# Memory attention in front of two expert layers: attention worked by whole batches instead of half batches

## The chip, the cores and the metric

One core of a Trainium2 chip runs the whole program. The metric is the device time of one execution in microseconds; lower is better. Times of a kernel are given as the median of several runs, and one further execution was profiled.

## What is computed

q, k and v have the shape (4 batches, 8 heads, 576 tokens, 64), phi has (4, 8, 576, 32). For each batch and head:

```
a    = softmax(phi, axis=2)                 # over the 576 tokens
k_m, v_m = a^T k, a^T v                     # 32 memory rows of 64
attn = softmax(q k_m^T / 8)                 # over the 32 memory rows
out  = attn v_m
```

The result, as 2304 tokens by 512, goes through a first layer (512 to 2048, leaky ReLU, back to 512; its weights are float64) and through a second one of 4 experts (512 to 1024, ReLU, back to 512), whose outputs are summed with the token's normalised domain probabilities as weights.

## The kernel before

**The order of the work.** The body does not issue instructions at once. It gives each operation to a planner (`Plan.op`, L52) with an engine, a cost in us, a due time, and the tiles and PSUM banks that it reads and writes. `Plan.issue` (L94) then simulates the engines with these costs, takes in each queue the operation that is ready and due first, and emits it. So each engine's order is fixed before the run, by costs and due times; at run time an engine works its list strictly in order. SP's list holds the DMA issues; it too is worked in order.

**Attention.** A group is 4 heads of one batch, so there are 8 groups, two for each batch (`att_group`, L519). Its steps: phi (L531 to L543: the whole group is transposed in 32x32 blocks by VectorE, the maximum over tokens is taken, ScalarE takes the exponential and the sum), a (L552: six TensorE transposes back to token layout and a copy), q (L558: a block transpose of the group's queries), kv (L569: 24 products of 96 tokens each), k (L581 to L601: scaling, transposes, copies), and scores (L615: 24 products, and then L627 to L651 on VectorE, ScalarE and GpSimd: block transpose, maximum, subtraction, exponential, sum, reciprocal, product, transpose back). At the end `split` (L335, L338) writes the tokens as a rounded high part and a remainder. q, k and v come in as one DMA each for a group: 96 partitions with 4 rows of 1536 bytes (6 tokens). phi comes in on 128 partitions with rows of 2304 bytes. The dues of the loads are in `LOADS` and `order` (L220, L672 to L697).

**First layer.** It runs in steps (`moe1_step`, L930): one step is a half batch (288 tokens) and 128 of the hidden columns. In a step there are 6 products on L895 (into the hidden layer), a leaky ReLU on L950, a `split`, and 12 products on L962 to L964 (out of the hidden layer, 4 of each line). What L895 multiplies with, the product of v_m and the weights, is made in `y_pair` (L897, matmuls on L911). The first unit covers 6 column chunks: for each batch 12 steps, six for the first 288 tokens and six for the other 288. The four batches of this unit come first, in order.

**Weights.** The float64 weights are turned into float32 on the chip, a piece of 128x512 values at a time (`piece64`, L782): ScalarE L795 and L799, VectorE L807 and L810, GpSimd L815 or L819, for w_out a `split` as well. A piece lands in one of three raw buffers (`RAWS`, L212; `raw_piece`, L716). A w_in piece is two DMAs of 64 partitions (L733). The first unit needs 6 pieces of w_in and 6 of w_out, 512 KB each.

**Idle products.** While TensorE has nothing to do in the first 50 us of the plan, the planner puts in products of the identity with itself (L471), whose results nobody reads.

**Tokens.** A token's column is (c, position) with 6 consecutive tokens on a row, so the probabilities and the result are moved with a stride, in two or three DMAs for each 128 tokens (L388, L1158).

Of the kernel before, what the change touches and what calls it, by code (L numbers as in the profile page):

```python
# [12 lines left out]
U32 = mybir.dt.uint32  # L13
# [162 lines left out]
def kernel(  # L176
# [197 lines left out]
    def rows_of(dram, b, c, lo, n):  # L374

        return dram[b * S:(b + 1) * S, :].rearrange("(p c) w -> c p w", c=NC)[c, lo:lo + n, :]

    def pieces(t):

        done = 0  # L380
        while done < P:
            b, s = divmod(t * P + done, S)
            c, lo = divmod(s, PC)
            n = min(P - done, PC - lo)
            yield done, b, c, lo, n
            done += n

    def load_probs(t):  # L388
        for at, b, c, lo, n in pieces(t):
            nc.sync.dma_start(out=pr[at:at + n, t, :], in_=rows_of(moe2_domain_probs, b, c, lo, n))  # L390
# [78 lines left out]
    def idle(bank):  # L469
# [5 lines left out]
    W = HG * NC * D  # L475
    pl = [tile_([NR, M]) for i in range(2)]
    ql = [tile_([HG, NC, D]), xx[:, 2, S:S + W].rearrange("p (h c d) -> p h c d", h=HG, c=NC)]
    kv = [tile_([2, HG, NC, D]), xx[:, 0:2, S:S + W].rearrange("p i (h c d) -> p i h c d", h=HG, c=NC)]
    eT = tile_([S])
    qT = [exact(HG, NC, 2, M), xx[:, 3, S:S + W].rearrange("p (h c e t) -> p h c e t", h=HG, c=NC, e=2)]  # L480
    kb = tile_([2, P])
    a = tile_([NC, P])
    kk = exact(2, NA3, M)
    vv = exact(2, D)
    at = [tile_([NR, M + 1]) for i in range(2)]
    aT = tile_([S])
    small = {
        nm: [tile_([n]) for i in range(2)]
        for nm, n in (("mx", NR), ("sm", NR), ("nmx", 1), ("z", 1), ("rz", 1))
    }  # L490
# [5 lines left out]
    memset(["vv"], vv)  # L496
    for i in range(2):
        memset([f"one{i}"], at[i][:, :, M:M + 1], 1e-9)

    def load(nm, t, src, i, due):  # L500

        b, g = divmod(i, NGB)
        hs = slice(g * HG, (g + 1) * HG)

        def fn():
            if nm[0:2] == "pl":
                nc.sync.dma_start(
                    out=t.rearrange("p r m -> p (r m)"),
                    in_=src[b, hs, :, :].rearrange("h (t r) m -> (h t) (r m)", t=M),
                )  # L510
            else:
                nc.sync.dma_start(
                    out=t[0:PC].rearrange("p h c d -> p h (c d)"),
                    in_=src[b, hs, :, :].rearrange("h (p c) d -> p h (c d)", c=NC),
                )

        plan.op("SP", 1.0 if nm[0:2] == "pl" else 2.0, due, fn, writes=[nm])

    def att_group(i):  # L519


        b, g = divmod(i, NGB)
        x = int(i in ALT)
        pl_ = pl[i % 2]
        nmx, z, rz, mx, sm = [small[nm][i % 2] for nm in ("nmx", "z", "rz", "mx", "sm")]
        at_ = at[i % 2]
# [4 lines left out]
        op("DVE", dve(S), due, lambda: nc.vector.transpose(out=eT, in_=pl_.rearrange("p r m -> p (r m)")),  # L531
           [f"pl{i % 2}"], ["eT"])
        op("DVE", dve(S), due, lambda: nc.vector.tensor_reduce(
            out=nmx, in_=eT, axis=AX.X, op=ALU.max, negate=True), ["eT"], [f"nmx{i % 2}"])
        op("ACT", 0.93, due, lambda: nc.scalar.activation(
            out=pl_.rearrange("p r m -> p (r m)").rearrange("p (c t r) -> p r c t", c=NC, r=NA3),
            in_=eT.rearrange("p (r c t) -> p r c t", r=NA3, c=NC),
            func=AF.Exp, bias=nmx, scale=1.0, accum_out=z),
           [f"nmx{i % 2}", "eT"], [f"pl{i % 2}", f"z{i % 2}"])

        def fn():
            nc.vector.tensor_scalar_add(rz, z, 1e-9)
            nc.vector.reciprocal(rz, rz)  # L543
        op("DVE", 0.3, due, fn, [f"z{i % 2}"], [f"rz{i % 2}"])

        due = yield
        pa = Banks(psum, 2)

        def fn():
            flat = pl_.rearrange("p r m -> p (r m)")  # L550
            for c in range(NC):
                nc.tensor.transpose(pa[c * P:(c + 1) * P][0:PC], flat[:, c * PC:(c + 1) * PC], ident)  # L552
        op("PE", 0.8, due, fn, [f"pl{i % 2}", "ident"], [pa], ["a"])
        op("ACT", act(NC * P), due, lambda e: copy(e, a[0:PC].rearrange("p c m -> p (c m)"), pa[0:NC * P][0:PC]), [pa], ["a"],
           also=("DVE", dve(NC * P)))

        due = yield
        op("DVE", 1.75, due, lambda: nc.vector.transpose(  # L558
            out=qT[x][0:PC].rearrange("p h c e t -> p (h c e t)"), in_=ql[x][0:PC].rearrange("p h c d -> p (h c d)")),
           [f"ql{x}"], [f"qT{x}"])  # L560

        due = yield
        pkv = Banks(psum, 1)

        def fn():
# [643 lines left out]
```

## Time and profile before

| what | us |
|---|---|
| median of 3 runs | 1163.4 (1161.43 to 1164.5) |
| the profiled execution, its own time | 1159.59 |
| its span, first to last instruction | 1157.8 |
| TensorE busy in the span | 1130.7 |
| mean granted TensorE clock | 0.991 |

The profiled execution is 3.8 us below the median of the runs. Busy time is the time in which an engine had at least one instruction under way; in the rows, L471 counts as busy too. In tables of stretches the granted clock is a share of full speed, and the DMA share is the mean busy share of the 16 DMA engines.

### The profile page before, as it was taken

What the parts mean: (1) busy time and instruction counts of PE and PEld (TensorE: products, weight loads), DVE (VectorE), ACT (ScalarE), POOL (GpSimd) and SP (SyncE); (2) the same over time, 40 slices, a digit from 0 to 9 for tenths busy, and PEclk for the clock granted to TensorE, in tenths of its full rate; (3) what the DMA queues carried; (4) which work ended last, traced back from release to release, by engine and by line L of the source; (5) the groups of instructions that cost most, each with busy time, mean ns of one, the idle gap of its engine ahead of it and who ended that gap; (6) DMA issues with size and microseconds to landing.
All of it is one profiled execution on the core that took longest, in us unless ns stands there. A gap on an engine that the chain in (4) does not pass through costs nothing.

```text
span 1157.8 us, 18008 instructions
## 1 busy us (share of the span) xinstructions
PE 1130.7 (98%) x7328; PEld 1028.5 (89%) x7328; DVE 687.2 (59%) x1259; ACT 446.6 (39%) x915; POOL 101.1 (9%) x102
## 2 busy tenths in 40 slices
PE   6799999999999999999999999999999999999998
PEld 6579899989999998889899989999998899999997
DVE  4887547853335788668686744445476654454543
ACT  4676557743344544433333423222224223222220
POOL 1542115420000000000000000000000000000000
PEclk8989999999999999999999999999999999999999
DMA  9974504410000267555534664334444553444402
GB/s 239 223 183 117 125 2 145 129 38 1 1 20 1 101 232 263 187 200 200 197 135 165 178 216 150 135 136 152 164 164 147 172 188 134 151 164 164 164 19 55
DMA packets 58836, 160.85 MB, mean 139 GB/s; under 512 B 6529, under 2 KB 33153, under 8 KB 52609
## 3 DMA queue, kind: packets, MB, share of 16 engines
q1 hardware_dynamic: 54144, 100.98, 28.4%
q0 software_dynamic: 4608, 58.72, 14.4%
q8 instruction: 57, 0.93, 0.3%
q14 instruction: 27, 0.21, 0.1%
HBM read 125.60 MB, written 34.08 MB: 138 GB/s over the span
## 4 chain that ended last, share of the span: by engine, by line
PE 92%; DMA 3%; DVE 2%; ACT 1%; POOL 1%; issue 1%; SPq 0%; POOLq 0%; ACTq 0%; DVEq 0%
PE psum L1070 30%; PE psum L1139 11%; PE psum L1140 11%; PE psum L1138 11%; PE psum L895 8%; PE psum L962 6%; PE psum L963 5%; PE psum L964 5%; PE psum L911 1%; DMA exact<-in_moe_w_out_dram 1%; DMA exact<-in_moe_w_in_dram 1%; PE psum L569 1%; DMA att<-in_v_dram 1%; PE psum L615 1%; PE psum L552 1%
## 5 line engine op out<-in xcount | busy, mean ns | idle before, releaser
L1079 DVE TENSOR_TENSOR exact<-psum,exact 128x384 f32<-128x384 f32 x336 | 184.3, 556 | 273.4 <-PE psum L1070 269.3
L1086 ACT ACTIVATE rounded<-exact 128x384 fp32r<-128x384 f32 x192 | 100.9, 525 | 286.0 <-DVE exact L1079 284.2
L338 DVE TENSOR_TENSOR rounded<-exact,rounded 128x288 fp32r<-128x288 f32 (+3 forms) x223 | 125.3, 579 | 102.6 <-ACT rounded L335 101.9
L1140 PE MATMUL psum<-late,rounded 128*128 128x512 f32 x384 | 150.7, 392 | 0.0
L1139 PE MATMUL psum<-late,rounded 128*128 128x512 f32 x384 | 150.5, 392 | 0.0
L1138 PE MATMUL psum<-late,rounded 128*128 128x512 f32 x384 | 149.3, 389 | 0.0
L1070 PE MATMUL psum<-rounded 128*128 128x384 f32 x768 | 143.5, 336 | 0.0
L1070 PEld LDWEIGHTS psum<-rounded 128*128 128x128 f32 x768 | 134.8, 188 | 2.5 <-DVE exact L1079 0.3
L895 PE MATMUL psum<-rounded 128*128 128x288 f32 x768 | 123.3, 298 | 1.5 <-DVE rounded L338 1.2
L335 ACT CAST rounded<-exact 128x288 fp32r<-128x288 f32 (+3 forms) x235 | 112.7, 497 | 16.6 <-DVE exact L757 5.5
L962 PE MATMUL psum<-rounded 128*128 128x288 f32 x384 | 116.3, 303 | 2.8 <-ACT exact L950 2.7
L895 PEld LDWEIGHTS psum<-rounded 128*128 128x128 f32 x768 | 108.9, 190 | 5.4 <-issue 3.5
L963 PE MATMUL psum<-rounded 128*128 128x288 f32 x384 | 113.4, 295 | 0.2 <-DVE rounded L338 0.2
L964 PE MATMUL psum<-rounded 128*128 128x288 f32 x384 | 113.4, 295 | 0.0
L1070 PE MATMUL psum<-late,rounded 128*128 128x384 f32 x576 | 110.1, 336 | 0.1
L1070 PEld LDWEIGHTS psum<-late,rounded 128*128 128x128 f32 x576 | 102.0, 188 | 4.4 <-DVE exact L1079 0.4
L1090 DVE SCALAR_TENSOR_TENSOR rounded<-exact,rounded 128x384 fp32r<-128x384 f32 x192 | 98.9, 551 | 11.5 <-ACT rounded L1086 11.4
L1101 ACT COPY exact<-psum 128x384 f32<-128x384 f32 x48 | 23.1, 481 | 195.7 <-PE psum L1070 195.7
L950 ACT ACTIVATE exact<-psum 128x288 f32<-128x288 f32 x128 | 52.5, 410 | 115.9 <-PE psum L895 102.3
L1140 PEld LDWEIGHTS psum<-late,rounded 128*128 128x128 f32 x384 | 72.0, 188 | 15.1
L962 PEld LDWEIGHTS psum<-rounded 128*128 128x128 f32 x384 | 72.3, 188 | 13.4 <-issue 9.2
L1139 PEld LDWEIGHTS psum<-late,rounded 128*128 128x128 f32 x384 | 72.0, 188 | 13.4
(101 smaller groups left out, 1701.5 us busy)
## 6 DMA issues: line engine op xcount, KB each, us to landing
rounded<-kept POOLq DMA_DIRECT2D x22, 1792.0 KB, 7.7
exact<-in_moe_w_dram SPq DMA_DIRECT2D x64, 512.0 KB, 5.1
kept<-rounded SPq DMA_DIRECT2D x10, 1792.0 KB, 6.7
w<-kept POOLq DMA_DIRECT2D x10, 1792.0 KB, 7.8
kept<-w SPq DMA_DIRECT2D x6, 1792.0 KB, 6.1
exact<-in_moe_w_in_dram SPq DMA_DIRECT2D x32, 256.0 KB, 5.9
exact<-in_moe_w_out_dram SPq DMA_DIRECT2D x16, 512.0 KB, 4.3
att<-in_q_dram SPq DMA_DIRECT2D x6, 576.0 KB, 5.8
```

The source lines that it names most:

```text
L335: nc.scalar.copy(out, in_) if e == "ACT" else engine(e).tensor_copy(out, in_)
L338: engine(e).tensor_tensor(out=out, in0=in0, in1=in1, op=ALU.subtract)
L895: nc.tensor.matmul(ps, lhsT=l, rhs=r, start=start and n == 0, stop=stop and n == len(seq) - 1)
L962: nc.tensor.matmul(po, lhsT=w2l[:, ds_], rhs=th, start=first, stop=False)
L963: nc.tensor.matmul(po, lhsT=w2h[:, ds_], rhs=tl, start=False, stop=False)
L964: nc.tensor.matmul(po, lhsT=w2h[:, ds_], rhs=th, start=False, stop=last)
L1070: nc.tensor.matmul(ps[k][0:TB], lhsT=l, rhs=r, start=(i == 0), stop=(i == 5))
L1079: plan.op("DVE", dve2(TB), at[k], lambda: nc.vector.tensor_tensor(out=o, in0=ps[k][0:TB], in1=other, op=ALU.add), [ps[k], ok, from_], [key])
L1086: plan.op("ACT", act2(TB), at[k], lambda: nc.scalar.activation(out=th, in_=src, func=AF.Relu), [key, *h_from[hs[c, i]]], [keys[0]])
L1138: nc.tensor.matmul(po[0:DM], lhsT=tl, rhs=w2h[:, c], start=(p == 0 and c == 0), stop=False)
L1139: nc.tensor.matmul(po[0:DM], lhsT=th, rhs=w2l[:, c], start=False, stop=False)
L1140: nc.tensor.matmul(po[0:DM], lhsT=th, rhs=w2h[:, c], start=False, stop=(p == NP2 - 1 and c == 1))
```

## The change

A batch is now worked as a whole. q, k, v and phi of a batch come in as one DMA each, on 128 partitions, with 9 tokens in a row (2304 bytes, for phi 1152). phi stays in token layout: the maximum is taken for each of the 32 columns of each partition, reduced over partitions by a TensorE transpose, spread back by a second transpose and subtracted; the sums over tokens come out of TensorE as products with two columns of ones. kv is 72 products of 64 partitions and 32 columns. Scores and all that follows are done for a half of the tokens (288) and all 8 heads at a time. k and v of most batches, and q of one, are loaded into the space that later holds the first layer's result (`xx`), and so the first layer's first result of a batch waits until that batch's space is free. Four more raw buffers (`MORE`) lie in the same space, where q and k of batch 1 are loaded later; those two loads wait for the readers of the four. A w_in piece is one DMA; probabilities and results are one DMA for 128 tokens. Dues and planner costs are new.

```diff
-    NC = 6
-    PC = S // NC
-    NA3 = PC // 32
+    LT = S // D
+    LP = P // H
-    RAWS = 3
+    RAWS, MORE = 3, 4
-    START = 40.0
-    URGENT = 40.0
+    START = 80.0
-    LOADS = [-69.0, -11.0, -9.5, 12.0, 24.0, 36.0, 48.0]
-    EACH = 2.5
-    ALT = (1, 3)
+    LOADS = [-59.9, 0.0, 10.0, 40.0]
+    PERIOD, LEAD, EACH, LAST = 32.0, 34.0, 3.0, -7.0
...
+    places = {"A": tile_([1, HG, S]), "X": xx.rearrange("p h (b s) -> p b h s", b=B)}
+    HOME = {"k": ["X0", "X3", "X1", "X3"], "v": ["X1", "X1", "X3", "X2"], "q": ["A0", "X2", "A0", "A0"]}
...
+        src, name = {"k": k, "v": v, "q": q}[what], HOME[what][b]
+        plan.op("SP", 3.5, due, lambda: nc.sync.dma_start(
+            out=home(name), in_=src[b].rearrange("h s d -> (h s d)").rearrange("(h p w) -> p h w", h=HG, p=P)),
+            writes=[name])
...
+        op("DVE", 1.25, due, lambda: nc.vector.tensor_reduce(
+            out=mr.rearrange("p (h m) -> p h m", h=HG), in_=a.rearrange("p h r m -> p h m r"), axis=AX.X, op=ALU.max),
+           [ka], ["mr"])
+        pm = Banks(psum, 1)
+        op("PE", 0.13, due, lambda: nc.tensor.transpose(pm[0:P], mr, ident), ["mr", "ident"], [pm])
+        op("DVE", 0.3, due, lambda: nc.vector.tensor_reduce(
+            out=nmx, in_=pm[0:P].rearrange("p (g t) -> p g t", g=NGB), axis=AX.X, op=ALU.max), [pm], [f"nmx{b % 2}"])
+        op("DVE", 0.25, due, lambda: nc.vector.tensor_copy(mb, nmx.unsqueeze(2).to_broadcast([P, NGB, D])),
+           [f"nmx{b % 2}"], ["mb"])
+        pb = Banks(psum, 1)
+        op("PE", 0.13, due, lambda: nc.tensor.transpose(pb[0:P], mb.rearrange("p g t -> p (g t)"), ident),
+           ["mb", "ident"], [pb])
+        op("DVE", 1.3, due, lambda: nc.vector.tensor_tensor(
+            out=a, in0=a, in1=pb[0:P].rearrange("p (h m) -> p h m", h=HG).unsqueeze(2).to_broadcast([P, HG, LT, M]),
+            op=ALU.subtract), [pb], [ka])
+        op("ACT", 1.2, due, lambda: nc.scalar.activation(out=pl[b % 2], in_=pl[b % 2], func=AF.Exp), [], [ka])
...
+        op("DVE", 2.5, due, lambda: nc.vector.transpose(
+            out=qT.rearrange("p h c e t -> p (h c e t)"), in_=home(qn)), [qn], ["qT"])
...
+                for r in range(LT * first):
+                    for h in range(HG):
+                        nc.tensor.matmul(
+                            pkv[2 * D:2 * D + NGB][h * M:(h + 1) * M], lhsT=a[:, h, r], rhs=ones,
+                            start=(r == 0), stop=(r == LT - 1),
+                        )
+                for r in range(LT):
+                    for h in range(HG):
+                        for g in range(NGB):
+                            gs = slice(g * D, (g + 1) * D)
+                            nc.tensor.matmul(
+                                pkv[g * 512:g * 512 + n * D][h * M:(h + 1) * M].rearrange("p (i d) -> p i d", i=n),
+                                lhsT=a[gs, h, r],
+                                rhs=src[gs, :, h, r * D:(r + 1) * D],
...
+        for s in range(2):
+            due = yield
+            at_, mx, sm, soon = at[s], small["mx"][s], small["sm"][s], b == s == 0
+            ps = Banks(psum, 2)
...
                 for e in range(2):
                     for h in range(HG):
-                        for j, w in enumerate(ws):
-                            rs = slice(w * M, (w + 1) * M)
+                        for g in range(NGB):
+                            rs = slice((2 * g + s) * M, (2 * g + s + 1) * M)
                             nc.tensor.matmul(
...
+                                rhs=qT[rs, h, :, e].rearrange("p r t -> p t r"),
...
+    STEP = ("phi", "q", "k", "s0", "s1")
+    STEP0 = ("phi", "k", "q", "s0", "v", "s1")
...
+            load(name[0], b, LOADS[b] + 0.1 * "pqvk".index(name[0]) - 200.0 * (name in ("p0", "k0")))
+    loads(["p0", "k0", "v0", "q0", "p1", "k1", "q1"])
...
+    for b in range(B):
+        plan.op("X", 0.0, 0.0, lambda: None, [], [f"free{b}"], room=[f"X{b}"])
...
+        if RAWS <= n < RAWS + MORE:
...
-                    after = ["alt"] if b else []
+                    after = [f"free{b}"]
...
-                    for at, b, c_, lo, n_ in pieces(tt):
...
+                    nc.sync.dma_start(out=out[tt * P:(tt + 1) * P, :].rearrange("n (k w) -> n k w", k=KD), in_=a_)
...
+    for x in range(MORE):
+        plan.ops[loaded["q1" if x < 2 else "k1"]][3].update({plan.writer[f"more{x}"], *plan.readers[f"more{x}"]})
```

## Rows read from the trace of the kernel before

**Rows 1.** The page: TensorE's busy time, and its busy tenths in 40 slices.

```profile
PE 1130.7 (98%) x7328; PEld 1028.5 (89%) x7328; DVE 687.2 (59%) x1259; ACT 446.6 (39%) x915; POOL 101.1 (9%) x102
...
PE   6799999999999999999999999999999999999998
```

**Rows 2.** Busy time by stretch: PE, PEld, DVE, ACT, POOL, clock, DMA share, GB/s.

```profile
0.00:72.00 72.00, 52.45 (x586) 44.54 (x587) 49.74 (x73) 40.87 (x79) 26.42 (x28) 0.88 1.00 240
72.00:100.00 28.00, 28.00 (x366) 24.66 (x365) 25.07 (x41) 21.34 (x48) 9.92 (x8) 1.00 0.45 105
...
160.00:440.00 280.00, 277.73 (x2118) 263.07 (x2117) 168.01 (x316) 144.54 (x312) 38.16 (x28) 1.00 0.23 75
440.00:1158.00 718.00, 712.50 (x3562) 642.60 (x3560) 412.94 (x779) 207.99 (x403) 17.16 (x32) 1.00 0.46 159
```

**Rows 3.** The same by stretch, for line 471 alone (PE, PEld, clock, DMA, GB/s).

```profile
0.00:72.00 72.00, 15.47 (x104) 14.07 (x104) 0.88 1.00 240
```

**Rows 4.** The same for line 895 alone.

```profile
0.00:72.00 72.00, 8.46 (x48) 7.60 (x48) 0.88 1.00 240
72.00:95.00 23.00, 5.17 (x33) 4.67 (x34) 1.00 0.39 91
```

**Rows 5.** The same for line 962 alone.

```profile
0.00:72.00 72.00, 7.15 (x22) 4.41 (x22) 0.88 1.00 240
72.00:95.00 23.00, 8.38 (x27) 4.88 (x26) 1.00 0.39 91
```

**Rows 6.** Waits of SP's queue up to 80 us: total, times, longest.

```profile
SPq L733 <- POOL w L815: 20.4, 5, 7.4
```

**Rows 7.** Timeline of SP: start, length, issues.

```profile
5.57 5.84 SPq L733 DMA_DIRECT2D exact<-in_moe_w_in_dram  x4
...
30.35 3.49 SPq L733 DMA_DIRECT2D exact<-in_moe_w_in_dram  x4
...
49.24 0.59 SPq L512 DMA_DIRECT2D exact<-in_v_dram  x1
```

**Rows 8.** Busy time by stretch, columns as in rows 2: three stretches that differ in row length.

```profile
58.00:60.00 2.00, 1.69 (x57) 1.17 (x56) 1.43 (x3) 0.26 (x1) 1.28 (x1) 0.80 1.03 379
2.00:4.00 2.00, 2.00 (x11) 2.00 (x10) 0.29 (x1) 0.24 (x1) 0.00 (x0) 1.00 0.88 299
10.00:16.00 6.00, 2.92 (x49) 2.56 (x50) 1.05 (x4) 0.07 (x1) 0.00 (x0) 0.62 1.11 242
```

**Rows 9.** Groups by line and shape up to 240 us: busy, mean ns, idle before.

```profile
L558 DVE STREAM_TRANSPOSE exact<-att 96x1536 f32<-96x1536 f32 x6 | 10.6, 1765 | 0.3 <-DMA att<-in_q_dram 0.3
...
L638 DVE TENSOR_REDUCE att<-att 128x18 f32<-128x576 f32 x8 | 6.0, 752 | 0.2
...
L807 DVE SCALAR_TENSOR_TENSOR exact<-exact 128x512 uint32<-128x512 uint32 x31 | 27.2, 876 | 1.3 <-ACT exact L799 0.4
...
L810 DVE TENSOR_SCALAR exact<-exact 128x512 uint32<-128x512 uint32 x32 | 25.8, 806 | 9.5 <-ACT exact L795 9.2
```

**Rows 10.** Groups by line and shape from 72 to 160 us: busy, mean ns, idle before.

```profile
L615 PE MATMUL psum<-exact,att 32*32 32x192 f32 x240 | 7.7, 326 | 0.0
...
L569 PE MATMUL psum<-att 96*32 96x128 f32 x192 | 6.1, 275 | 0.0
...
L552 PE MATMUL psum<-att 128*96 128x128 f32 x24 | 3.3, 272 | 0.0
```

**Rows 11.** Timeline of TensorE: start, length, matmuls.

```profile
13.09 2.79 PE L569 MATMUL psum<-att 96*32 96x128 f32 x48 [4.22 <-DMA att<-in_v_dram]
...
68.39 0.95 PE L895 MATMUL psum<-rounded 128*128 128x288 f32 x6
```

**Rows 12.** Timeline: first and last operation of group 0's softmax.

```profile
19.62 1.07 DVE L627 STREAM_TRANSPOSE att<-psum 128x384 f32<-128x384 f32 x2 [2.44 <-PE psum L615]
...
27.14 1.42 POOL L338 TENSOR_TENSOR rounded<-att,rounded 128x576 fp32r<-128x576 f32 x1 [1.60 <-ACT rounded L335]
```

**Rows 13.** Timeline of TensorE: the first product of the first layer.

```profile
36.39 1.81 PE L895 MATMUL psum<-rounded 128*128 128x288 f32 x12 [1.16 <-DVE rounded L338]
```

More of the change, by code (lines that the diff above doesn't have):

```diff
@@ L369, in pool @@
         return 0.1 + n * 2.33e-3
[L374 to L386, printed above, removed]
     def load_probs(t):
-        for at, b, c, lo, n in pieces(t):
-            nc.sync.dma_start(out=pr[at:at + n, t, :], in_=rows_of(moe2_domain_probs, b, c, lo, n))
+        nc.sync.dma_start(out=pr[:, t, :], in_=moe2_domain_probs[t * P:(t + 1) * P, :])
     def norm_probs():
@@ L527, in att_group, with att_batch @@
+    def att_batch(b):
+        a = pl[b % 2].rearrange("p h (r m) -> p h r m", r=LT)
+        nmx, rz = [small[nm][b % 2] for nm in ("nmx", "rz")]
+        qn = HOME["q"][b]
+        ka = f"pl{b % 2}"
         op = plan.op
         due = yield
[L531 to L534, printed above, removed]
@@ L546, in att_group @@
-        due = yield
[L547 to L557, printed above, removed]
@@ L657, in att_group @@
-        rest((0, 1))
-        if i == ALT[-1]:
-            plan.op("X", 0.0, due, lambda: None, [], ["alt"], room=["ql1", "kv1k", "kv1v", "qT1"])
-        yield
-    LATER = {i: next((j for j in range(i + 1, NG) if (j in ALT) == (i in ALT)), NG) for i in range(NG)}
-    FIRST = (
[3 rows of a table removed]
-    )
-    STEP = (("kv", 0), ("phi", 1), ("k", 0), ("scores", 0), ("a", 1), ("q", 1))
-    order = []
-    for what, i in FIRST + tuple((what, i + n) for i in range(2, NG) for what, n in STEP if i + n < NG):
-        order.append((what, i))
-        for after, then in (("kv", "lk"), ("kv", "lv"), ("q", "lq")):
-            if what == after and LATER[i] < NG:
-                order.append((then, LATER[i]))
-        if what == "a" and i + 2 < NG:
-            order.append(("lp", i + 2))
@@ new lines, in loads @@
+    def loads(names):
+        for name in names:
+            b = int(name[1])
+            loaded[name] = len(plan.ops)
+            load(name[0], b, LOADS[b] + 0.1 * "pqvk".index(name[0]) - 200.0 * (name in ("p0", "k0")))
+    loads(["p0", "k0", "v0", "q0", "p1", "k1", "q1"])
+    for b in range(B):
+        step = STEP if b else STEP0
+        for n, what in enumerate(step):
+            if b:
+                due = PERIOD * b - LEAD + n * EACH
+            else:
+                due = n / len(step) * START - 2 * START if n < len(step) - 1 else LAST
+            gens[b].send(due)
+            loads(AFTER.get((what, b), ()))
@@ L809, in signs, with add @@
                 )
+        def add(e, out):
+            cuts = [(slice(i, i + 1),) for i in range(2)] if e == "DVE" and rk[0] == "m" else [()]
+            for cut in cuts:
+                cut = (every, *cut)
+                engine(e).tensor_tensor(out=out[cut], in0=fu[cut], in1=low[cut], op=ALU.add)
         plan.op("DVE", 0.42, due, lambda: nc.vector.tensor_single_scalar(fu, fu, 3, op=ALU.logical_shift_left),
```

316 lines of the change are left out of this document (139 added, 177 removed), and 3 rows, old and new, of the table FIRST.

## The prediction

> **What bounds the kernel now.** The page comes first: TensorE is busy for 98% of the span, and only the first two of the 40 slices are below 9 tenths [rows 1]. The table by stretch says the same more sharply. From 72 us on TensorE has no gap worth the name: all of 72 to 100, 277.73 of 280 us up to 440, and 712.50 of 718 after that; up to 72 it is busy for 52.45 [rows 2]. Of these, 15.47 are idle products [rows 3], so about 37 of the first 72 us are work, at a mean clock of 0.88. The ramp is thus the only place where anything much can be won, and what is won there reaches the end one for one, because after it TensorE alone sets the pace.
>
> How far is TensorE at 72 us? Batch 0's 12 steps have 72 products on L895 and 48 on L962. At 72 us 48 and 22 of them are done [rows 4, 5]; between 72 and 95 another 27 of L962 follow. So batch 0 is through at about 95 us. I use that as the milestone: when does the new kernel have batch 0 done and batch 1's tokens ready?
>
> What holds the ramp? The DMA engines are full: share 1.00 and 240 GB/s over the first 72 us [rows 2], some 17 MB. SP's queue adds its own delay: weight loads wait 20.4 us for GpSimd to finish with one of three raw buffers [rows 6], and behind them, in the same list, stand the inputs of the next groups. The first weight loads go out at 5.57 us behind all of batch 0's inputs, and the last v of batch 1 goes out only at 49.24 [rows 7]. VectorE is the next in line: 25.07 of 28 us from 72 to 100 [rows 2], while it does nothing for most of 10 to 16 us (1.05 of 6) [rows 8].
>
> **The change part by part.**
> Transfers. Rows of 1536 bytes come in at 242 GB/s (10 to 16 us), phi's 2304-byte rows at 299, the 4 KB rows of w_out at 379 [rows 8]. q, k and v of a batch are 3.54 MB: 14.6 us before, 11.8 at the rate of phi's rows. phi's own rows shrink to 1152 bytes; no row shows that, so I bound it by 299 (no loss) and half of it (2 us lost on 0.59 MB), and take 0.8 lost, nearer to the 242 of the next larger rows. Net 2 us a batch. The Trainium skill ("DMA: Bandwidth & Descriptors", Rules for kernel authors) asks for 128 partitions and at least 1 MiB in a DMA for full bandwidth; its table (Measured) gives 341 GB/s for 1 MB, which would make it 10.4 us a batch. In the rows 96 partitions already keep all engines full (1.11), so I hold to the length of the row; the rest is a rival.
>
> Order of the loads. By the new dues phi and k of batch 0 go first, then three weight pieces, then q and v, then four weight pieces into the new buffers without waiting, and only then batch 1. So weights can be converted while VectorE and ScalarE used to stand idle, and the 20.4 us of waiting in SP's list go at least for these pieces. What is late next is batch 1, whose q and k now wait for the readers of the four buffers.
>
> VectorE. L638 shows 752 ns for 576 columns, L558 1765 for 1536 [rows 9]. A group before: seven passes of 576 columns (L531, L533, both L627 together, L638, L639, L643, L651) 5.3, the query transpose 1.8, small ones 0.8: 7.9 us, 15.8 a batch. Now: a maximum over 1152 columns 1.5, subtraction 1.5, query transpose 2304/1536 x 1.765 = 2.65, small ones 0.9, and twice (five passes of 576 plus a reciprocal, 4.0) = 14.6. The strided maximum and the subtraction with a PSUM operand are in no row; at worst they take double, 3 us more. Six block transposes and copies for phi fall away on ScalarE, about 4 us a batch; they were beside other work and count for nothing alone.
>
> TensorE. A group now has 24 calls on L569 and 24 on L615, 48 records each, and nine transposes. The records take 7.7/240 = 6.1/192 = 32 ns each, a transpose 3.3/24 = 0.14 us [rows 10]. A batch before: 192 x 0.032 + 18 x 0.14 = 8.7. Now, at two records a call: sums 72, kv 144, scores 64, the new small transposes 20: 300 x 0.032 + 2 x 0.14 = 9.9. So TensorE pays about 1.2 us more a batch. The ends: sums of two columns may be cheaper (1 us less), scores read with a stride of 64 elements may take double (2 us more). In batches 2 and 3 this lies on the path: +2.4 us. With a low clock a record takes 2.79/48 = 58 ns [rows 11], as would batch 0's.
>
> Walk through the start. With transfers running from 2 us on at 240 to 300 GB/s, phi of batch 0 is in at about 4.5 us and k at 8.5. The phi chain (two passes of 1152 columns, 3.0; four small steps, 1.2; the exponential, taken as one more pass, 1.5; 1 for handing over, an estimate) ends at 11. 216 records for k take 7 to 12.5 us: 18 to 23.5; scaling, transposing and copying 2 more. q comes behind 4.5 MB, at 19, and its transpose ends at 22. Scores of the first half: 24 to 27. Group 0's softmax goes from 19.62 to 28.56 now [rows 12], 8.9 us; with its product on VectorE instead of GpSimd about 8. So the first tokens are ready at 32 to 35; I take 33. Today the first product of the first layer starts at 36.39 [rows 13], and then it runs out of weights.
>
> From 33 us TensorE needs, to the milestone: 72 + 144 products of batch 0 at (0.95 - 0.29)/5 = 0.131 us [rows 11], 28.3; 48 records of L911 at 32 ns, 1.5; batch 1's attention, 9.9. Without a wait that ends at 73. VectorE needs: two attentions 29.2, less 4 for batch 1's second half, 12 weight pieces at 0.806 + 0.876 [rows 9] = 20, 12 steps and three pairs at 0.6 = 9; 54 in all, of which 15 are done by 33. The other 39 at the 90% that it reaches from 72 to 100 take 43: 76. I take 77, a little later than both.
>
> Sum: 95 - 77 = 18 us earlier at the milestone. From that goes what the old kernel has done besides by 95: 9 products of L895 (81 against 72), 1.2, and the start of batch 2's attention, 2.5. Then 2.4 for dearer attention. 18 - 3.7 - 2.4 = 12 us. Fewer issues for probabilities and results lie beside other work: nothing. Made against the profiled execution's 1159.6 that gives 1147.6; that execution is 3.8 below the median of the runs, 1163.4, and against the median I predict 1151.4.
>
> **The rivals.**
> (a) The ramp stays bound by the DMA and the conversions: the same bytes, only 4 us quicker for two batches, and weight pieces 8 to 12 still wait for three raw buffers. For it: the share of 1.00; against it: TensorE needs all 14 MB of batches 0 and 1 and the first weights only by the milestone, not by 60 us. Milestone at 86: 95 - 86 - 3.7 - 2.4 = 3 us, 1160.4.
> (b) Slower: batch 1's q and k come too late. They stand in SP's list behind the last weight pieces and wait for the readers of four buffers; then 1.18 MB each, the kv products, and the softmax of 8 us follow, with TensorE empty after batch 0's 12 steps. It decides if batch 1's first tokens are ready later than 95 - 3.7 - 2.4 = 89 us. If the two loads go out at 65 instead of the 45 to 50 I expect, they land at 75, kv and scores end at 83 and tokens come at 95 or, with VectorE as full as it is, 97: 8 us lost, 1171. Against it: the four buffers are among the first to be converted.
> (c) Larger gain: the big transfers run like w_out's rows, 379 GB/s. 9.3 us a batch instead of 11.8, first tokens at 30, TensorE without waits: milestone 70, 95 - 70 - 6.1 = 19 us, 1144.4. This is where the skill's rule on large transfers would lead, too.
>
> **How the numbers follow.** The forecast has 0.60, (a) 0.14, (b) 0.13, (c) 0.13. With the milestone between 71 and 83, the forecast itself reaches from 1145 to 1157; the unknown costs add 2 to 4 us a batch at worst. The range takes in (a) and most of (c): 1142 to 1162; outside lie (b) and little else. 0.3% is 3.5 us, about what a measurement of this kernel can tell from no change. Faster by more: the forecast, (c) and a third of (a), 0.78; within it 0.09; slower 0.13.
>
> **What would show it.** Right: the first product on L895 at 31 to 35 us, the 48th of L962 before 80, TensorE near full from about 40 us, and q/k/v transfers at some 300 GB/s. The DMA share falling under 1 before 60 us would show that order, not bytes, held the ramp. Wrong: a gap of TensorE between batch 0 and batch 1 that ends with L627's tokens (then b), waits of L962 for converted weights until 60 us (then a), or matmuls of the attention at over 40 ns a record.

## The result and the profile after

The changed kernel takes 1179.85 us (median of 4 runs, 1178.73 to 1180.41); the kernel before, run beside it, 1162.41 (1159.8 to 1164.5). The ratio is 1.015, with an interval of 1.0126 to 1.0173: 17.4 us slower, where 11 to 12 us less was forecast. The profiled execution took 1179.85 us, with a span of 1177.9.

First the page of the kernel after: busy time of each engine, and TensorE's busy tenths in 40 slices.

```profile
PE 1146.6 (97%) x7852; PEld 1033.5 (88%) x7852; DVE 681.9 (58%) x1238; ACT 436.0 (37%) x889; POOL 98.9 (8%) x101
...
PE   6689999999999999999999999999999999999998
```

Against [rows 1], TensorE is busy for 15.9 us longer (1146.6 against 1130.7), and the span has grown by 20.1. So only 4.2 us of the difference are gaps; the rest is TensorE at work, and the question is with what. Next the table by stretch (columns as in rows 2):

```profile
0.00:72.00 72.00, 48.47 (x735) 38.27 (x739) 40.60 (x50) 29.28 (x52) 22.59 (x27) 0.88 0.64 228
72.00:100.00 28.00, 27.25 (x365) 21.02 (x360) 17.35 (x27) 15.40 (x36) 10.35 (x8) 0.83 0.56 188
...
160.00:440.00 280.00, 280.00 (x2272) 262.99 (x2259) 158.38 (x300) 146.69 (x322) 39.47 (x28) 1.00 0.16 54
```

Against [rows 2], the DMA engines are no longer full in the first 72 us (0.64 instead of 1.00), VectorE has done 40.60 us instead of 49.74, and TensorE 48.47 instead of 52.45. The ramp has lost its old bound and is longer all the same. The milestone says how much; the same table for the first of the three products of the second matmul (L951, which was L962):

```profile
0.00:72.00 72.00, 4.54 (x12) 2.69 (x12) 0.88 0.64 228
72.00:95.00 23.00, 4.29 (x13) 2.70 (x13) 0.79 0.68 229
```

25 products by 95 us stand against 49 in [rows 5]. Batch 0 is through after 110 us, when the 48th has started.

What else TensorE does in the whole span stands in its groups by line (busy time, mean ns of one record, idle before). First the lines of attention and of the idle products in the kernel before:

```profile
L471 PE MATMUL psum<-att 128*128 128x128 f32 x104 | 15.5, 300 | 1.4 <-POOL att masks.py:199 1.4
...
L615 PE MATMUL psum<-exact,att 32*32 32x192 f32 x384 | 11.9, 326 | 2.2 <-ACT att L335 2.2
L569 PE MATMUL psum<-att 96*32 96x128 f32 x288 | 10.4, 299 | 4.5 <-DMA att<-in_v_dram 4.2 <-ACT att L335 0.3
L552 PE MATMUL psum<-att 128*96 128x128 f32 x48 | 8.6, 330 | 3.9 <-ACT att L535 3.9
...
L595 PE MATMUL psum<-att,exact 128*96 128x128 f32 x16 | 3.4, 295 | 0.5 <-ACT exact L581 0.5
L569 PE MATMUL psum<-exact,att 96*32 96x128 f32 x96 | 3.0, 274 | 0.3 <-DMA exact<-in_v_dram 0.3
L596 PE MATMUL psum<-att,exact 128*128 128x128 f32 x8 | 2.3, 291 | 0.0
```

And the same in the kernel after (L610 scores, L453 idle products, L548 and L540 products and sums, the others transposes):

```profile
L610 PE MATMUL psum<-att,exact 32*32 32x288 f32 x256 | 23.3, 764 | 0.0
L453 PE MATMUL psum<-att 128*128 128x128 f32 x116 | 21.1, 347 | 1.4 <-POOL att masks.py:199 1.4
...
L548 PE MATMUL psum<-exact,att 64*32 64x128 f32 (+1 forms) x720 | 13.8, 285 | 7.0 <-issue 7.0
...
L540 PE MATMUL psum<-att 128*32 128x2 f32 x288 | 3.5, 178 | 2.7 <-ACT att L525 2.7
L590 PE MATMUL psum<-att,exact 128*32 128x128 f32 x64 | 3.0, 314 | 0.0
L586 PE MATMUL psum<-att,exact 128*64 128x128 f32 x16 | 1.8, 298 | 0.0
L520 PE MATMUL psum<-att 128*128 128x128 f32 x4 | 1.4, 350 | 0.2 <-DVE att L517 0.2
L514 PE MATMUL psum<-att 128*128 128x128 f32 x4 | 1.3, 337 | 3.0 <-DVE att L510 3.0
```

Attention took TensorE 39.6 us before (the six rows without L471) and takes 48.1 now. Scores alone went from 11.9 to 23.3. The idle products grew by 5.6: there are 116 instead of 104, at 347 ns instead of 300.

These rows give the account that the rest of this text uses. **Work** is TensorE's busy time without the idle products; **rest** is the span without the work, that is gaps and idle products together. Before: 1130.7 - 15.5 = 1115.2 of work, 42.6 of rest. After: 1146.6 - 21.1 = 1125.5 and 52.4. So of the 20.1 us, 10.3 are dearer work and 9.8 are rest. The rest has grown in the first 160 us alone, from 35.1 to 47.7; after that the changed kernel has 3 us fewer gaps. So this part is a longer ramp. (Records overlap: the mean of 764 ns is not what one costs; a group's busy time is nearer to it. For the same reason the subtraction leaves out a little too much where idle products lie between others, so work and rest are compared only between kernels that both have idle products, or both have none.)

**Why scores are dear.** TensorE's timeline (start, length, records, idle before):

```profile
11.92 1.47 PE L548 MATMUL psum<-exact,att 64*32 64x64 f32 x121
17.80 0.65 PE L548 MATMUL psum<-exact,att 64*32 64x64 f32 x23 [4.41 <-issue]
...
24.11 2.79 PE L610 MATMUL psum<-att,exact 32*32 32x288 f32 x32
...
28.42 3.54 PE L610 MATMUL psum<-att,exact 32*32 32x288 f32 x32
```

32 records take 2.79 and 3.54 us, 87 and 111 ns each, against 32 ns for records of 192 columns in [rows 10]: 1.5 times the columns, about 3 times the time. The granted clock is 1.00 in all three stretches, so the clock is not the reason.

**Who waits.** Waits up to 72 us (VectorE's up to 100), in all, times, longest:

```profile
DVE att L618 <- PE psum L610: 11.6, 4, 4.8
...
ACT exact L782 <- DMA exact<-in_v_dram: 5.9, 1, 5.9
...
POOL w L802 <- DVE exact L794: 17.5, 3, 11.4
POOL exact L802 <- DVE exact L794: 17.0, 1, 17.0
POOL exact L802 <- DMA exact<-in_q_dram: 6.8, 1, 6.8
POOL w L802 <- DMA exact<-in_v_dram: 4.5, 1, 4.5
...
SPq L495 <- POOL exact L802: 10.8, 1, 10.8
...
SPq L495 <- DVE exact L794: 7.9, 2, 5.7
```

SP's timeline (start, length, issues) has the three loads of batch 1:

```profile
42.19 0.37 SPq L495 DMA_DIRECT2D exact<-in_v_dram  x1
49.38 0.37 SPq L495 DMA_DIRECT2D exact<-in_q_dram  x1
...
61.70 0.37 SPq L495 DMA_DIRECT2D exact<-in_k_dram  x1
```

VectorE waits 11.6 us for scores. And a thing that makes no sense by the data: L782 and L802 are steps in the conversion of weight pieces, and they wait for loads of batch 1's v and q. Those loads are late themselves: before they go out at 42.19 and 49.38, SP has waited 7.9 us for VectorE's passes of earlier conversions (L794). Batch 1's k follows only at 61.70, after 10.8 us of waiting for GpSimd's (L802). What these waits cost is seen in two stretches (columns as in rows 2):

```profile
45.00:50.00 5.00, 0.99 (x16) 0.20 (x8) 0.94 (x2) 2.49 (x5) 1.71 (x1) 0.73 0.38 148
...
55.00:60.00 5.00, 1.17 (x11) 0.97 (x9) 1.70 (x3) 2.06 (x6) 3.87 (x3) 1.00 0.75 286
```

TensorE is busy for 2.2 of these 10 us, VectorE for 2.6.

### The profile page after: what moved, and what is told of

Same layout as the page of the kernel before. It is cut to its first block, busy times and chain, and to the rows that moved or that the text cites. A ratio compares the mean times of both kernels' runs of the same rounds, so it can differ in the third digit from the quotient of the medians.

```text
span 1177.9 us, 18878 instructions
## 1 busy us (share of the span) xinstructions
PE 1146.6 (97%) x7852; PEld 1033.5 (88%) x7852; DVE 681.9 (58%) x1238; ACT 436.0 (37%) x889; POOL 98.9 (8%) x101
## 3 DMA queue, kind: packets, MB, share of 16 engines
q0 software_dynamic: 4608, 58.72, 14.1%
## 4 chain that ended last, share of the span: by engine, by line
PE 95%; DVE 1%; DMA 1%; issue 1%; ACT 1%; POOL 0%; POOLq 0%; SPq 0%; DVEq 0%
PE psum L1059 30%; PE psum L1129 11%; PE psum L1128 11%; PE psum L1127 11%; PE psum L884 9%; PE psum L951 6%; PE psum L953 6%; PE psum L952 6%; PE psum L610 2%; PE psum L900 1%; PE psum L548 1%; PE psum L453 1%; DMA exact<-in_q_dram 1%; DMA exact<-in_v_dram 0%; DVE exact L794 0%
## 5 line engine op out<-in xcount | busy, mean ns | idle before, releaser
L884 PE MATMUL psum<-rounded 128*128 128x288 f32 x768 | 125.4, 300 | 2.2 <-DVE rounded L335 2.2
L951 PE MATMUL psum<-rounded 128*128 128x288 f32 x384 | 116.1, 302 | 6.0 <-POOL rounded L335 5.6
L884 PEld LDWEIGHTS psum<-rounded 128*128 128x128 f32 x768 | 110.1, 191 | 9.2 <-issue 5.6
L951 PEld LDWEIGHTS psum<-rounded 128*128 128x128 f32 x384 | 72.8, 190 | 18.7 <-issue 10.7
L1128 PEld LDWEIGHTS psum<-late,rounded 128*128 128x128 f32 x384 | 72.0, 188 | 13.4
```

The source lines that it names most:

```text
L884: nc.tensor.matmul(ps, lhsT=l, rhs=r, start=start and n == 0, stop=stop and n == len(seq) - 1)
L951: nc.tensor.matmul(po, lhsT=w2l[:, ds_], rhs=th, start=first, stop=False)
L1128: nc.tensor.matmul(po[0:DM], lhsT=th, rhs=w2l[:, c], start=False, stop=False)
```

## The experiments

All runs in one table. The ratio is to the kernel before in the runs beside it, with its interval; span, work and rest are those of the profiled execution, as worked out above.

| kernel | median us | ratio to before | span | work | rest |
|---|---|---|---|---|---|
| before | 1160 to 1163 | 1 | 1157.8 | 1115.2 | 42.6 |
| after | 1179.85 | 1.015 (1.0126 to 1.0173) | 1177.9 | 1125.5 | 52.4 |
| e1 scores contiguous | 1166.2 | 1.0038 (1.0023 to 1.0054) | 1164.2 | 1110.5 | 53.7 |
| e2 loads after conversions | 1170.35 | 1.0079 (1.0063 to 1.0095) | 1169.9 | 1122.0 | 47.9 |
| e3 both | 1162.55 | 1.0016 (1.0005 to 1.0026) | 1160.5 | 1110.5 | 50.0 |
| e4 transfers halved | 1193.57 | 1.0281 (1.0261 to 1.03) | 1191.2 | 1125.1 | 66.1 |
| e5 = e3, honest costs | 1158.26 | 0.9975 (0.9961 to 0.9989) | 1158.5 | 1111.1 | 47.4 |
| e6 = e3, no idle products | 1160.69 | 1.0001 (0.9986 to 1.0016) | 1158.4 | 1118.2 | 40.2 |
| e7 = e1, three buffers | 1162.8 | 1.001 (0.9998 to 1.0022) | 1161.3 | 1111.3 | 50.0 |
| e8 = e5 and e6 | 1156.38 | 0.9956 (0.9941 to 0.9972) | 1153.1 | 1115.0 | 38.1 |
| e9 = e8, less VectorE work | 1155.51 | 0.995 (0.9933 to 0.9967) | 1153.4 | 1115.3 | 38.1 |
| e10 = e8, three buffers | 1155.69 | 0.9952 (0.9937 to 0.9967) | 1152.8 | 1116.5 | 36.3 |
| c1 = before, no idle products | 1159.95 | 0.9992 (0.9974 to 1.001) | 1156.0 | 1122.1 | 33.9 |

### e1: scores read in the order in which they lie

```diff
-    ps[g * 512:g * 512 + HB][h * M:(h + 1) * M].rearrange("p (t r) -> p t r", t=M),
+    ps[g * 512:g * 512 + HB][h * M:(h + 1) * M].rearrange("p (t r) -> p r t", t=M),
...
-    rhs=qT[rs, h, :, e].rearrange("p r t -> p t r"),
+    rhs=qT[rs, h, :, e],
```

In `qT` the 32 values of one r and one e lie side by side, and the next r is 64 elements further. The changed kernel reads with r innermost, so each value is 64 elements from the last. e1 reads along the row and does the reordering where the result is written, in PSUM.

> Edit: in the scores the moving operand is read with its 32 tokens side by side, as the kernel before did, and the new token order is made in the write to PSUM instead. Theory A (the strided read of the scores costs): the 256 records on this line fall from 23.3 us busy to about 12, each half from 2.8 us to about 1.3, and since VectorE stood 4.8 and 2.4 us waiting for batch 0's scores, the ramp shortens too: 1179.9 goes to 1164 to 1170. Theory B (waits for loads in the ramp decide): the scores fall as well, but the gaps of TensorE at 45 to 50 and 55 to 60 us stay, and only the part after 100 us is won, some 5 us: 1173 to 1176. Rival C (writing to PSUM with a stride of 9 costs as much as reading with one of 64): no change, 1180.

Measured: 1166.2, 13.7 us less than the changed kernel. From TensorE's timeline in e1:

```profile
23.63 1.24 PE L610 MATMUL psum<-att,exact 32*32 32x288 f32 x32
```

1.24 us for 32 records, 39 ns each, instead of 87 to 111, again at a granted clock of 1.00. The scores fall from 23.3 to 11.1 us in all, and VectorE's waits for them up to 100 us from 11.6 to 5.6. Work falls by 15.0 us, to 1110.5, and rest stays (53.7). So the stride is the dear thing, and it is dear on the reading side: a stride in the writing of PSUM (nine floats apart) costs so little that a column is cheaper than before (39/288 against 32/192 ns). The Trainium skill ("SBUF — State Buffer", Door 1: The DMA port swizzle) says that SBUF is read in lines of 16 bytes and that each access to a new line pays. The trace agrees as far as a read step of 256 bytes goes: it costs 2.2 to 2.8 times the time here.

### e2: the loads of batch 1 after the conversions

```diff
     for x in range(MORE):
-        plan.ops[loaded["q1" if x < 2 else "k1"]][3].update({...})
+        for nm in ("v1", "q1", "k1"):
+            plan.ops[loaded[nm]][3].update({...})
```

No engine's work changes; batch 1's three loads are merely held until all four added buffers have been read.

> Edit: the loads of batch 1's q, k and v all go out after the conversions of all four added raw buffers, so no conversion stands behind such a load. Theory B: VectorE, ScalarE and GpSimd no longer wait for v's transfer at 47.5 us and q's at 56, TensorE's gaps at 45 to 50 and 55 to 60 (10 us) go, but batch 1's inputs land some us later: 1179.9 goes to 1170 to 1175. Theory A: the conversions stand behind VectorE's wait for the scores in any case; within 3 us of 1180.

Measured: 1170.35, 9.5 us less than the changed kernel, though v and q of batch 1 go out later (at about 53 us; k at 60.4). The two kinds of wait for `in_v` and `in_q` at L782 and L802 are gone from the list of waits. The stretches of e2:

```profile
45.00:50.00 5.00, 4.76 (x47) 3.98 (x45) 4.93 (x9) 4.28 (x10) 3.22 (x3) 1.00 0.45 162
...
55.00:60.00 5.00, 2.77 (x13) 2.53 (x14) 4.73 (x5) 0.00 (x0) 3.21 (x3) 0.74 1.04 404
```

TensorE's 2.2 us in the two empty stretches have become 7.5. So the waits held the ramp. By the data they were not needed: the buffers lie in the third and fourth quarter of each row of the tile, v of batch 1 in the second, with no byte in common; and q, which takes the place of two of them, goes out only after their readers, by the change's own rule, so no conversion needs it. That they arise because an access with steps is taken for everything between its first and last byte is an inference from which instructions waited; no run shows it directly.

### e3: both

> Both edits, contiguous scores and loads after the conversions. If A and B are separate, their gains add: 1157 to 1165. If they are the same time seen twice (a conversion waits for the scores or for the load, whichever ends later), the sum is no better than the larger of the two alone plus 3 us.

Measured: 1162.55, 17.3 us less than the changed kernel, where the single gains add up to 23.2: some 6 us of the loss are behind both waits, so that either edit wins them. The loss is explained, for e3 is within 0.16% of the kernel before. But the forecast gain is not there either. Work is 4.7 us below before, and rest 7.4 above it.

### e4: the big transfers in two halves

q, k, v and the float64 weight pieces are loaded as two transfers, partitions 0 to 63 and 64 to 127. The length of the rows is unchanged.

```diff
-    nc.sync.dma_start(out=home(name), in_=src...)
+    for i in range(2):
+        ps = slice(i * D, (i + 1) * D)
+        nc.sync.dma_start(out=home(name)[ps], in_=src...[ps])
```

> Edit: each load of q, k, v and of the float64 weights is cut into two of 64 partitions with the same rows. If the rate of 390 GB/s between 5 and 25 us comes from transfers over 128 partitions, it falls to 240 to 300 GB/s and the first ten transfers end about 8 us later. If it comes from the length of a row (2304 bytes for 1536), it stays at 385 or above. On the time: the transfers from 5 to 25 us are not what the ramp waits for later, so at most 5 us more than 1180 either way.

Measured: 1193.57, 13.7 us more, all of it in the rest (66.1 against 52.4), so the expectation of at most 5 was too low; so was that of 240 to 300 GB/s. The stretch from 5 to 25 us, first in e2, whose transfers are those of the changed kernel:

```profile
5.00:25.00 20.00, 14.51 (x290) 12.59 (x298) 8.55 (x11) 5.42 (x9) 2.59 (x2) 1.00 1.05 391
```

and then in e4:

```profile
5.00:25.00 20.00, 10.51 (x260) 9.21 (x261) 8.05 (x11) 5.81 (x9) 2.58 (x2) 0.85 1.06 221
```

391 and 221 GB/s with the same rows, and the DMA share is the same: a full share says that the engines have work, not that they move bytes at their best. The kernel before, with 96 partitions and shorter rows, stood at 242 [rows 8]. A half is also a smaller transfer, 576 KB; but w_out's pieces of 512 KB, on 128 partitions, came at 379 in the kernel before [rows 8], so the size alone is not the reason. The Trainium skill ("SBUF — State Buffer", Door 1: The DMA port swizzle) gives a reason: partitions 0 to 63 lie behind 8 of 16 ports, which carry about 218 GB/s. The 221 agree.

### e5: the planner's costs as measured

On e3. The order of every engine's list comes from costs that the changed kernel had put too low: a phi maximum at 1.25 us (measured 2.1 to 2.2), batch 0's products at 1.5 for k (7 us with the pause described below).

```diff
-        op("DVE", 1.25, due, lambda: nc.vector.tensor_reduce(
+        op("DVE", 2.1, due, lambda: nc.vector.tensor_reduce(
...
-            op("PE", 0.9 + 0.6 * len(names), due, ...)
+            op("PE", (7.2 if "k" in names else 1.7) if b == 0 else 3.4, due, ...)
...
-            op("PE", 0.9, due, fn, ["qT", "kb"], [ps], [f"at{s}"])
+            op("PE", 1.25, due, fn, ["qT", "kb"], [ps], [f"at{s}"])
```

> On top of contiguous scores and later loads: the planner is given the measured costs (kv of batch 0's k 7.2 us instead of 1.5, its v 1.7, later kv 3.4 instead of 2.1, scores 1.25 instead of 0.9, maximum over phi 2.1 instead of 1.25). Nothing that is computed changes, only the order of each engine's list. Theory D (what is left of the ramp's loss is that weight conversions stand in the lists behind attention steps that come later than planned): SP's pause from 22 to 37 us shrinks below 8 us, the first product on L884 stays near 36, the products follow more closely, and 1162.5 goes to 1152 to 1159. Rival: VectorE, busy for 27.7 of the 30 us from 30 to 60, is full in any order: within 3 us of 1162.5.

Measured: 1158.26, 4.3 us less than e3. The pause in SP's list that was to shrink is still there (17 to 34 us), and the first product on L884 comes at 38.2 instead of 36.9 in e3. So the gain has another source than expected, which stays open; VectorE is busy for 29.15 of the 30 us from 30 to 60, after 27.69 in e3.

### e6: no idle products

On e3.

```diff
-    WARM, PART, IDLE, SHORT = (3.0, 50.0), 0.5, 0.22, 0.5
+    WARM, PART, IDLE, SHORT = (3.0, 0.0), 0.5, 0.22, 0.5
```

> On top of contiguous scores and later loads: no idle products. Theory E (TensorE's pause of 4.5 us in the middle of batch 0's kv products, without any wait in the profile, is the supply of instructions): it comes at a place in the instruction stream, so with 14 idle products fewer ahead of it, it moves some 14 calls further on, out of the 72 kv products and into the transposes or the scores, and is still there. If instead it hangs on the data of kv, it stays after the 121st record on L548. On the time: the clock in the first 40 us falls to 1.2 GHz more often, which costs 1 to 4 us; no product is held up by an idle one, which gives 1 to 2: 1161 to 1166.

Measured: 1160.69, 1.9 us less than e3, though the intervals of the two ratios still overlap. So 21.5 us of idle products cost about 2 us: nearly all of them fill waits. The clock did not fall as expected: in the first 30 us the granted clock is 1.00 here and 0.93 in e3, from 30 to 72 us 0.80 and 0.81. And the pause moves. In e6's timeline:

```profile
12.33 2.27 PE L548 MATMUL psum<-exact,att 64*32 64x64 f32 x144
15.45 0.64 PE L590 MATMUL psum<-att,exact 128*32 128x128 f32 x4 [0.84 <-ACT exact L574]
18.37 1.07 PE L590 MATMUL psum<-att,exact 128*32 128x128 f32 x12 [2.28 <-issue]
```

The 144 products that stopped after 121 in the changed kernel run through, and TensorE stops further on. With the idle products gone, the same number of instructions reaches further into the work. Counted from the start, the stop comes after the 223rd of TensorE's products in the changed kernel and after the 222nd here; it ends at 17.8 us there and at 18.4 here.

### e7: e1 with three raw buffers

```diff
-    RAWS, MORE = 3, 4
+    RAWS, MORE = 3, 0
```

> Contiguous scores, and no added raw buffers at all (MORE = 0), with the loads of batch 1 where the change puts them. Theory B (conversions wait for loads only because the four buffers lie in the same tile as the loads): conversions no longer wait for the loads of v and q, as with the later loads, and the time is at or below 1162.5, or, if the four buffers by themselves shorten the ramp, between that and the 1166.2 of contiguous scores alone. If it is above 1167, the buffers are worth more than the waits that they bring, and B is only half of it.

Measured: 1162.8, 3.4 us less than e1 and level with e3. Without the four buffers there is nothing to wait for falsely, and nothing is lost with them.

### e8: all that helped, and e9, e10 beside it

e8 has the edits of e3, e5 and e6.

> All that the experiments found worth something in one kernel: contiguous scores, loads of batch 1 after the buffers' conversions, the honest planner costs (1158.3) and no idle products (1.9 us in the pair measured). Theory A+B+cost+place (the gains are separate stretches of the ramp and add up): 1156 to 1157, so 4 to 6 us below the kernel before. Rival (the ramp is held by VectorE, which was busy for 29.15 of the 30 us from 30 to 60 in the kernel with honest costs; what TensorE gains before 30 us is only waited for later): 1158 to 1159, no different from the kernel with honest costs.

Measured: 1156.38, ratio 0.9956 (0.9941 to 0.9972): the gains add up, and this kernel beats the one before by 5 us. With e10 below it is the fastest version found that computes everything.

In e9 the sign pass of the first 14 pieces is cut to 8 or 16 columns, so it leaves out the signs of the low halves of the other values:

```diff
-        low, high = raw[..., 0::2], raw[..., 1::2]
+        low, high, c = raw[..., 0::2], raw[..., 1::2], slice(0, 8 if npiece[0] <= 14 else None)
...
-                    out=low, in0=high, scalar=0x80000000, in1=low, ...
+                    out=low[..., c], in0=high[..., c], scalar=0x80000000, in1=low[..., c], ...
```

> The kernel of the line above with VectorE's sign pass over the first 14 weight pieces cut from 512 columns to 8 or 16 (the signs of the low halves of those weights are left out, so the output is not the reference's); every engine's order of instructions is the same. That takes 0.7 to 1.2 us from VectorE for each piece, 10 to 13 us in the first 80 us. Theory V (VectorE's list is what holds the ramp, once scores and loads are mended): 4 us or more below the kernel of the line above. Rival (the chain of loads, ScalarE or GpSimd's additions holds it, and VectorE is merely full): under 1.5 us less.

Measured: 1155.51, 0.9 us less than e8 and within the noise, so the rival held: VectorE is nearly full in the ramp, and still not what sets its end alone. The test is weaker than planned, since it took only 6.2 us from VectorE in the first 160 us instead of 10 to 13, and so it cannot rule out that VectorE holds a part. The timelines show why. e8:

```profile
41.99 0.68 DVE L794 SCALAR_TENSOR_TENSOR exact<-exact 128x512 uint32<-128x512 uint32 x1
...
46.09 1.75 DVE L794 SCALAR_TENSOR_TENSOR exact<-exact 128x512 uint32<-128x512 uint32 x1
```

e9, the same two instructions:

```profile
42.49 0.17 DVE L794 SCALAR_TENSOR_TENSOR exact<-exact 128x16 uint32<-128x16 uint32 x1
...
47.45 1.23 DVE L794 SCALAR_TENSOR_TENSOR exact<-exact 128x16 uint32<-128x16 uint32 x1
```

512 columns take 0.68 us or 1.75, 16 columns 0.17 or 1.23. The difference, 1.07 and 1.06, does not depend on the columns, which points to a wait inside the instruction. In e9 a product on GpSimd ran from 46.07 to 47.25 and a subtraction from 47.20 to 48.64, the end of which is that of the 16 columns (47.45 + 1.23 = 48.68). In both kernels that subtraction ends 1.19 us after the slow instruction began. The Trainium skill ("SBUF — State Buffer", Who interferes with whom) calls what VectorE and GpSimd share an exclusive lock; the two pairs agree.

e10 is e8 without the four buffers (the edit of e7).

> The kernel of the first line without the four added raw buffers, so that all early pieces go through three. Theory B in its full form (the buffers only did harm, by the waits that they made): the same within 2 us as with them, 1156 to 1159. Rival (with the loads held back until after the conversions the buffers do now feed the first steps earlier): 3 us or more slower than with them.

Measured: 1155.69, within 0.7 us of e8. So the buffers are worth nothing even where nothing waits falsely.

### c1: the kernel before without idle products

The edit of e6, in the kernel before.

> The kernel before, without its idle products (15.47 us of TensorE's busy time in the first 72 us). It tells whether the 5 us by which the mended kernel without idle products (1156.4) beats the kernel before (1161.3) come from the change at all. Theory (the idle products fill waits there and cost next to nothing, so the 5 us are the change's): within 1.5 us of the kernel before. Rival (they cost the kernel before what they cost the mended one, about 2 us): 1159 to 1160, and only 3 us of the 5 are the change's. A third possibility, that they pay by keeping the clock up: 2 us or more slower.

Measured: 1159.95 against 1160.52 beside it, ratio 0.9992 (0.9974 to 1.001). So most of the 5 us of e8 are not those of the idle products; the rival's 2 us still lie within the interval. Between c1 and e8, neither of which has them, work falls by 7.1 us and rest grows by 4.2: the same direction as between before and e3 (4.7 less, 7.4 more). The granted clock of the first 72 us is 0.79 in c1 and 0.95 in e8, so a part of the 7.1 may be the clock's.

## Why the prediction was wrong

**Scores (the term of the sum that was mis-sized).** The prediction counted scores at 32 ns a record and noted that "scores read with a stride of 64 elements may take double (2 us more)". They took 87 to 111 ns, and 23.3 us in all: 5.8 a batch instead of the 2 that were counted. Batches 0 and 1 were taken to lie in the ramp, where this would cost nothing; but there VectorE waits for the scores, 6.0 us longer than in e1. e1 gives 13.7 us back. The risk was seen, and its price taken from the wrong side: no row of before has such a read, and the bound of double was a guess with no row under it.

**The four buffers (a step that failed).** The step "four weight pieces into the new buffers without waiting" was right for the loads and false for what follows: their conversions waited for batch 1's v and q. Rival (b) had this place, but the other direction, q and k of batch 1 waiting for the conversions until 65 us. Of that a half came: q went out at 49.4, but k at 61.7, since the four buffers were not "among the first to be converted". What (b) priced, TensorE empty after batch 0's 12 steps, did not come: batch 0 itself lasted until 110 us, and from 72 to 100 us TensorE has hardly a gap (27.25 of 28). e2 gives 9.5 us back, 3.7 of them beyond e1 (1166.2 to 1162.55). Of the signs named for "wrong", two came: attention over 40 ns a record, and conversions still awaited until 60 us.

**Transfers (wrong the other way).** The prediction held the rate to the length of a row and set 299 GB/s; measured are 391 over 5 to 25 us. That 96 partitions "already keep all engines full (1.11)" was the wrong reading of the share: e4 shows the same share at 221. Rival (c), at 379, had the rate nearly right. The prediction set the rule of the Trainium skill ("DMA: Bandwidth & Descriptors", Rules for kernel authors), 128 partitions and at least 1 MiB, aside; e4 agrees with its first half. Yet (c) forecast 1144.4, and even e8 is far from it: with a DMA share of 0.64 in the first 72 us (0.72 in e8) the transfers had stopped being the bound.

**TensorE's attention (wrong in sign, once scores are mended).** Counted were 8.7 us a batch before and 9.9 after. The groups give 39.6/4 = 9.9 before and 48.1/4 = 12.0 after; with scores mended (e3) the same groups give 32.6/4 = 8.2, and the work falls to 1110.5, 4.7 us under that of before in all. Transposes were undercounted: 14.3 us before (L552, L595, L596) against 7.5 after. And 32 ns a record was too much for the small products: 13.8/720 = 19 ns on L548 and 3.5/288 = 12 ns on L540.

**The start (right, then late).** "Scores of the first half: 24 to 27" came at 24.11 to 26.90. The maximum took 2.1 to 2.2 us instead of 1.5, and the products stopped for 4.4 us where none was counted; what paid for both is that the 216 products themselves took 2.9 us (0.77, 1.47 and 0.65) instead of 7 to 12.5. The softmax then took from 27.07 to 37.44 instead of 8 us, because the lists of VectorE and ScalarE have steps ahead of its end that wait for TensorE until 32 us. The tokens were to be ready at 33; the first product on L884 starts here:

```profile
38.79 1.82 PE L884 MATMUL psum<-rounded 128*128 128x288 f32 x12 [2.23 <-DVE rounded L335]
```

**The walk to the milestone (the step that the runs refute).** 15 of VectorE's 54 us were to be "done by 33", since "weights can be converted while VectorE and ScalarE used to stand idle". VectorE had 12.2 us by 33 in the changed kernel and 14.1 in e8, so little is missing there. Still the idle time was not used: up to 33 us VectorE stands idle three times, for 5.5, 4.8 and 2.4 us, waiting for TensorE, and starts two sign passes, at 12.3 and 19.1. ScalarE, whose passes come first in a conversion, works on two pieces by 13.4 us and on the third at 33.1. Each engine takes its list in order, and the next conversions stand behind attention's next operation. GpSimd's one long wait of 17.0 us for VectorE is the same thing.

More is missing afterwards. From 33 us to the milestone VectorE was given 39 us of work at 90%, 43 us in all. In e8, where the 48th product of L951 starts at 92.3 us, it stands so (columns as in rows 2):

```profile
33.00:92.00 59.00, 44.99 (x577) 38.03 (x578) 48.39 (x63) 37.19 (x73) 29.20 (x23) 0.94 0.62 216
```

VectorE does 48.4 us of work, not 39 (a little of it for batch 2 already), and is busy for 82% of 59 us, not for 90% of 43. So the milestone moves neither in e8 (92 us) nor in e3 (96), where the kernel before has it at 93, and does not come to 77. From 30 to 60 us VectorE is busy for 27.69 (e3), 29.15 (e5) and 29.11 us (e8). Rival (a) had the conversions as the bound, but for want of raw buffers; e7 and e10, with three, lose nothing by them.

So the direction was wrong by two things that cost 17.3 us together and were priced at 2 us a batch outside the sum and at nothing; and without them the forecast would have been wrong still, by the 12 us of a shorter ramp that no mended kernel shows. e8 gains 5. What exactly ends the ramp in e8 stays open: it is not VectorE's busy time alone (e9), nor the raw buffers (e10), and an order with conversions ahead of the waits was not tried. One candidate was not tested: TensorE's stops without a wait in the profile. In e8 there are two, and the longer lies on the chain of work that ended last, ahead of batch 0's scores:

```profile
24.50 0.45 PE L548 MATMUL psum<-exact,att 64*32 64x64 f32 x12 [4.16 <-issue]
```

## What to carry to other kernels

Price an operand by how it lies, not by its shape: a change of layout that saves transposes can hand the cost to a strided read, and if no row shows such a read, its upper bound is open. A buffer placed in a tile that others also load into can be waited for though no byte is shared; look, in the waits, for a releaser that has nothing to do with the reader. And a full DMA share is no proof of a full rate: compare GB/s between transfers that differ in partitions as well as in row length.

## What the runs showed of the hardware that was not expected

- A strided read of TensorE's moving operand in fp32 (step 256 bytes): 87 to 111 ns for a record of 288 columns, against 39 ns along the row; a strided write into PSUM (step 36 bytes) shows no such loss.
- 128, 96 and 64 partitions: 391, 242 and 221 GB/s, all at a share over 1 (rows of 2304 bytes, with 96 partitions 1536).
- TensorE stops for 4.4 us amid 144 small products, with nothing in the profile that it waits for ("issue"). The stop follows the 223rd of TensorE's products in the changed kernel, in e1 to e5 and in e7, and the 222nd in e6, e8 and e10, which have no idle products, whatever the work is at that place. It ends between 17.8 and 18.5 us in all of these but e4, whose transfers are slower: there it ends at 21.3, after 7.1 us. In e5, e8 and e10 a second stop of 4.2 to 4.4 us comes 128 products later. So it goes with the place in the list of instructions, at a time when the DMA engines are full; that the instructions themselves arrive late over the same engines is likely, and only argued.
- An instruction on VectorE of 16 columns takes 0.17 us, or 1.23 beside a subtraction on GpSimd.
- Leaving out the idle products changed the granted clock either way and the time by little: between the kernel before and c1 it fell from 0.88 to 0.75 (30 to 72 us), at a ratio of 0.9992; between e3 and e6 it rose from 0.93 to 1.00 in the first 30 us, with 1.9 us less.
